# A written-out order of 758 operations over five engines, replaced by another order of the same operations

## The chip, the cores and the metric

The kernel runs on one core of a Trainium2 chip. The metric is the time of one execution on the device in microseconds (us), of which the median of several runs counts; beside it stands one execution taken by the hardware profiler, whose span runs from the first to the last instruction. Five engines work side by side: TensorE (PE in the rows, its weight loads PEld), VectorE (DVE), ScalarE (ACT), GpSimd (POOL) and SyncE (SP), which here only issues transfers. Each engine takes its instructions strictly in the order in which they stand in its own queue and waits at the first whose data or buffer is not ready.

## The reference

Two layers over 2048 positions and 640 channels are computed apart, and their outputs stand side by side (bf16).

```python
# A: a diagonal complex state-space layer
Bu = einsum("bld,pd->blp", x, B_bar)
for t in range(L): h = Lam_bar * h + Bu[:, t]; hs.append(h)
yA = 2 * einsum("blp,dp->bld", stack(hs), Cmat).real + x * Dskip
# B: a short convolution, a product, a long convolution, a gate
k_shift = sum of 4 shifted copies of k, each times a weight per channel
kv = k_shift * v
yB = q * (causal_conv(kv, ssm_k) + kv * ssm_D)     # by FFT in the reference
```

## The kernel before

The kernel builds a list of 758 operations (`build`, over the classes `PartA` and `PartB`). An operation is one instruction on DVE, ACT or POOL, one transfer on SP, or a block of matmuls on PE that fills a group of the eight PSUM banks; PE blocks are always followed by one eviction on DVE or ACT, which frees the banks. Nothing is scheduled at run time. A string, ORDER, lists every operation once as number, engine letter (T for PE, V for DVE, A for ACT, G for POOL, S for SP) and first PSUM bank. `Program.emit` goes through that string and puts each operation on its engine's queue; where an operation reads or overwrites what another engine wrote, a wait is set on that one. So the string decides three things: the order in each queue, which engine does an operation that several could do, and which banks a block takes.

The buffers are fixed places in one array and most are used several times. Those that matter here:

- KT holds one 128-channel plane of k at a time, so the load of the next plane (line 769) waits for the last of the four taps of the one before.
- VT holds three planes of v. Its first columns are scratch for two sine tables before that, so the first load of v waits for the ScalarE sine of line 304.
- KV holds one half (320 channels) of the product k_shift * v, spread anew; H0 holds first the first half of the filter ssm_k, then the scan of part A, then the second half of the filter, then half of q.

Part A. The input is projected in blocks by 512-column matmuls on PE: `up2`, `up1` and `up0` (lines 554 to 620, ten, five and fifteen groups), which reduce 16 consecutive positions to one. A coarse scan over 128 steps runs in two halves on DVE (`coarse`, lines 640 to 660; each half needs two small PE blocks, L646 and L647, and ends with the addition of line 660). Then the states go down again (`down`, L677 and L679, the addition by DVE at L697, or by an identity matmul L677 with a copy by ACT at L695). The output matrix is scaled on PE into CT (`scale_C`, ten blocks, L544, evicted at L548); it needs the two transposed loads of C (L530). Then 16 row blocks are projected (`project`): a load of x (L705), a product with Dskip (L706, DVE or POOL), 20 matmuls of 320 columns (L714, called a projection below), an addition on DVE (L716) and a store (L720).

Part B, in two halves. For each of five planes of 128 channels, k and v are loaded transposed (L769), four taps are multiplied (L197 on DVE, L198 on ACT) and added (L795), the sum is multiplied with v (L796), and the plane is stored to a scratch tensor in HBM, `kv_rows` (L802). The *relay* reads half of that back in the other layout with four transfers (L812). The filter half is loaded by four transfers (L762) and gets ssm_D added (L764). Both then go through a two-stage transform on PE: stage one (`s1`, L832, ten blocks, evicted at L837), stage two (`s2`, L850, eleven or twelve blocks, evicted at L863). The products of the two transforms run on DVE and POOL in four rounds per half (lines 874 to 881; each half's last line-879 subtraction is the end of its products). The inverse goes through `r2` (L895, ten blocks per half, evicted at L900) and `r1` (L916, six blocks per half), whose results are multiplied with the loaded q (L780) by DVE at L928 and stored (L940). Sine tables for the transforms are made early or late on POOL (integer products, L288 and L327) and ACT (L293, L329), and scaled at L197 or L198.

Of the kernel before, what the change touches and what calls it, by code (L numbers as in the profile page):

```python
# [1030 lines left out]
def plain_order(P):  # L1031
# [19 lines left out]
    "135S0 6G0 0G0 7V0 123A0 48V0 84V0 108G0 82V0 458V0 73G0 460G0 459V0 122A0 11V0 50S0 1G0 134S0 42G0 2V0 18G0 8V0 120T4 461G0 "  # L1051
    "20V0 49S0 51S0 121T3 127S0 115G0 12V0 9V0 71G0 26V0 470G0 45V0 44V0 14V0 19V0 21V0 43V0 124T6 126S0 10V0 471G0 53T4 54V4 125V6 "
    "55A0 4A0 114S0 56V0 163T1 137S0 15G0 3V0 74G0 63V0 72G0 64V0 109G0 65V0 119V0 46V0 16V0 57V0 66V0 136S0 60A0 67V0 62A0 85V0 "
    "59A0 87V0 47A0 68V0 5V0 86V0 61A0 69V0 70V0 165T3 75G0 164A1 76G0 77G0 330S0 78G0 79G0 110G0 80A0 58A0 22A0 167T0 166V3 133S0 "
    "81V0 465G0 25V0 104V0 175T6 168A0 33G0 132S0 24V0 118A0 27V0 105V0 333A0 177T2 128S0 332V0 83V0 91V0 28V0 269V0 23V0 334V0 "
    "173T0 129S0 178A2 335V0 176A6 88V0 336V0 331S0 199T2 29V0 89V0 337A0 34G0 90V0 174A0 30G0 169T5 341S0 92V0 94V0 338V0 31G0 "
    "200A2 112A0 179T1 141S0 339V0 170A5 36G0 35A0 116S0 171T4 180A1 93V0 138S0 96V0 343V0 37G0 344A0 52S0 183T2 342S0 101A0 172A4 "
    "345V0 39G0 107V0 191T6 346A0 139S0 40G0 117S0 38A0 347V0 140S0 215T4 32A0 111G0 130S0 41A0 184V2 348A0 181T0 216V4 131S0 192A6 "
    "142V0 466G0 349V0 352S0 157T2 182A0 155T4 207T6 156A4 475G0 158A2 340S0 106V0 145T4 208A6 153T2 185T0 353S0 154V2 146A4 350V0 "
    "355A0 354V0 151T6 224S0 149T4 186A0 95V0 356V0 201T2 152A6 100A0 357V0 97V0 358V0 187T0 202A2 193T6 359V0 98A0 188A0 150A4 "  # L1060
    "102V0 360V0 392S0 99A0 103V0 189T0 194A6 203T2 223S0 190A0 195T6 361V0 204A2 147T4 196A6 143T0 148A4 197T6 144V0 267G0 205T2 "
    "198A6 161T4 206A2 395V0 159T6 270T0 160A6 394V0 217T2 362S0 17V0 396V0 162A4 113A0 397V0 393S0 209T4 398V0 218A2 268V0 271V0 "
    "399V0 272V0 219T2 403S0 210A4 400V0 239T0 220A2 229T6 240A0 221T2 273V0 230A6 231T0 274V0 222A2 211T4 351S0 232A0 241T2 212A4 "
    "237T6 242A2 401V0 213T4 363S0 238A6 233T2 214A4 277V0 243T0 234A2 275T6 406V0 225T4 244A0 276V6 227T2 226A4 235T0 228V2 279T6 "
    "365S0 236A0 249T4 278V0 364S0 245T0 281V0 250A4 280V6 259T2 246A0 260V2 247T4 366S0 265T6 248A4 251T0 405V0 257T2 252A0 266V6 "
    "253T4 402S0 254A4 282V0 261T0 258V2 262A0 255T5 283V0 263T2 256A5 264A2 371T0 407V0 369T6 375T4 372A0 385T2 370V6 376A4 284T0 "
    "386A2 285V0 379T4 288T6 286V0 380A4 381T0 287V0 373T2 408V0 289A6 387S0 374V2 382A0 389S0 409G0 367T6 377T4 368A6 378V4 383T2 "
    "292T0 384A2 683S0 388S0 290T6 293A0 414T4 291V6 440T2 415A4 418T6 441V2 416T0 390S0 419A6 447T4 410V0 425T2 417A0 448V4 429T6 "
    "684G0 426A2 436T0 678S0 430V6 404S0 437A0 438T3 420V0 427T5 439A3 294T7 449T0 428A5 295V7 296T2 422V0 450A0 391V0 423V0 498T6 "
    "297A2 502T0 421V0 484T4 503A0 685T2 431V0 485A4 424V0 499A6 433V0 488T6 686V2 434G0 451T0 489A6 490T4 452V0 687S0 302T2 491A4 "  # L1070
    "298T0 303V2 494T6 299A0 500T4 495A6 496T0 411V0 680T2 703S0 497A0 693S0 679V0 566S0 501A4 412V0 462A0 442V0 413S0 486T0 492T4 "
    "463A0 695T6 567S0 694V0 487A0 444V0 681V2 493A4 445V0 464A0 544T2 696V6 568S0 304T0 569S0 545A2 453V0 308T4 305A0 562T6 309V4 "
    "697S0 550T2 454G0 563A6 560T0 682S0 551A2 561V0 546T4 548T6 547A4 556T2 549V6 554T0 557A2 443G0 558T4 555V0 552T6 713S0 559A4 "
    "564T2 688S0 553A6 565V2 572T0 584T4 573V0 580T6 585A4 455G0 570T2 581V6 571A2 586T0 300T4 587A0 576T2 301V4 306T6 577A2 476G0 "
    "574T0 307V6 588T4 575A0 578T2 457V0 582T6 589A4 715T0 579A2 714V0 432V0 583A6 456V0 435G0 590T4 716V0 627T6 591A4 592T2 628V6 "
    "717S0 594T0 698S0 593A2 623T4 595V0 605T6 624A4 689V0 601T2 603T0 446V0 606A6 316T4 596V0 472A0 690T6 602A2 317V4 604A0 704V0 "
    "467A0 598V0 612T2 614T0 599V0 700T4 615A0 691V6 477A0 607V0 613A2 699V0 324T0 701V4 616T2 325A0 597V0 702S0 625T6 312T4 609V0 "
# [79 lines left out]
```

## Time and profile before

| | |
|---|---|
| median of three runs | 216.62 us (212.32 to 216.9) |
| the profiled execution's own time | 211.25 us |
| its span, first to last instruction | 209.5 us |
| busy share: PE, DVE, ACT, POOL | 87%, 82%, 69%, 33% |
| mean granted TensorE clock | 0.957 of full speed |

The span is shorter than the execution's own time by 1.75 us of start and end around it. All that is read below in microseconds from the start belongs to this one execution.

### The profile page before, as it was taken

How to read it: one execution, taken by the hardware profiler on the slowest of the kernel's cores; microseconds unless marked ns; L12 is line 12 of the kernel's file. 1: busy time of each engine (PE TensorE's matmuls, PEld its weight loads, DVE VectorE, ACT ScalarE, POOL GpSimd, SP SyncE). 2: the span in 40 equal slices, each digit the busy share in tenths (PEclk: the TensorE clock that was granted, in tenths of full speed). 3: DMA queues.
4: the chain of work that ended last, by engine and by line, in shares of the span. 5: the costliest groups of instructions: out<-in, count | busy, mean ns of one | idle time of the engine just before them, and what ended most of it. 6: DMA issues, size and time to landing. Idle time of an engine off the chain costs nothing.

```text
span 209.5 us, 8273 instructions
## 1 busy us (share of the span) xinstructions
PE 181.4 (87%) x3727; PEld 119.0 (57%) x3727; DVE 172.4 (82%) x228; ACT 145.1 (69%) x171; POOL 68.4 (33%) x56
## 2 busy tenths in 40 slices
PE   4699999969999998398769996899999998999960
PEld 1345544524667556376546765576666777677740
DVE  5917998995799999687978997989999989787630
ACT  2099799776959599799957997989889988000000
POOL 8672099950002000016404039450036016102220
PEclk9969999996999999969969999999999999999995
DMA  7999969999999899819961998211096993147685
GB/s 139 176 153 166 199 136 154 159 147 147 223 192 212 234 253 131 173 18 152 136 119 38 210 149 126 69 39 30 34 156 157 186 195 97 35 113 205 156 195 157
DMA packets 107550, 30.20 MB, mean 144 GB/s; under 512 B 102395, under 2 KB 106875, under 8 KB 107515
## 3 DMA queue, kind: packets, MB, share of 16 engines
q1 hardware_dynamic: 107226, 29.35, 81.0%
q8 instruction: 29, 0.48, 1.0%
q10 hardware_dynamic: 288, 0.33, 0.6%
q14 instruction: 7, 0.05, 0.1%
HBM read 10.99 MB, written 7.86 MB: 90 GB/s over the span
## 4 chain that ended last, share of the span: by engine, by line
PE 32%; DMA 20%; DVE 14%; SPq 11%; POOL 5%; issue 4%; ACT 3%; DVEq 0%; ACTq 0%
PE acc L714 16%; DMA arena<-kv_rows 7%; DMA arena<-in_B_ssm_k_dram 6%; DVE arena L795 4%; DMA kv_rows<-arena 4%; PE acc L832 4%; DMA arena<-in_A_x_dram 3%; DVE arena L197 3%; PE acc L679 3%; PE acc L916 3%; SPq L705 2%; POOL arena L288 2%; SPq L762 2%; PE acc L850 2%; PE acc L554 2%
## 5 line engine op out<-in xcount | busy, mean ns | idle before, releaser
L554 PE MATMUL acc<-arena 128*64 128x512 bf16 x400 | 50.5, 407 | 1.6 <-DVE arena L504 1.0
L714 PE MATMUL acc<-arena 128*128 128x320 bf16 x320 | 46.6, 302 | 0.0
L714 PEld LDWEIGHTS <-arena 128*128 128x128 bf16 x320 | 30.5, 99 | 12.8 <-ACT arena L863 0.4
L554 PEld LDWEIGHTS <-arena 128*64 128x64 bf16 x400 | 23.1, 113 | 25.6 <-issue 4.0
L837 ACT CAST arena<-acc 128x1024 bf16<-128x1024 f32 x33 | 31.6, 1026 | 6.7 <-PE acc L832 6.6
L863 ACT CAST arena<-acc 128x960 bf16<-128x960 f32 (+1 forms) x33 | 29.7, 947 | 2.2 <-PE acc L850 1.8
L832 PE MATMUL acc<-arena 64*64 64x64 bf16 x1280 | 15.9, 202 | 11.3 <-DVE arena L764 5.3
L198 ACT ACTIVATE arena<-arena 128x1024 bf16<-128x1024 bf16 (+3 forms) x17 | 21.0, 1242 | 4.4 <-DVE arena L795 4.2
L850 PE MATMUL acc<-arena 128*64 128x160 bf16 x512 | 22.0, 235 | 2.1 <-ACT arena L863 1.0
L832 PEld LDWEIGHTS <-arena 64*64 64x64 bf16 x1280 | 13.4, 114 | 16.3 <-issue 4.9
L850 PEld LDWEIGHTS <-arena 128*64 128x64 bf16 x512 | 17.8, 109 | 6.9 <-ACT arena L863 3.6
L795 DVE TENSOR_TENSOR arena<-arena 128x2048 bf16<-128x2048 bf16 x14 | 20.0, 1429 | 0.7 <-ACT arena L198 0.5
L716 DVE TENSOR_TENSOR arena<-acc,arena 128x640 bf16<-128x640 f32 x16 | 13.2, 823 | 8.4 <-PE acc L714 5.5
L706 POOL TENSOR_TENSOR arena<-arena 128x640 bf16<-128x640 bf16 x6 | 9.2, 1540 | 32.9 <-DMA arena<-in_A_x_dram 32.9
L877 POOL TENSOR_TENSOR arena<-arena 128x1280 bf16<-128x1280 bf16 x4 | 10.3, 2608 | 24.9 <-DVE arena L874 24.9
L900 ACT CAST arena<-acc 128x1024 bf16<-128x1024 f32 x15 | 14.7, 1026 | 1.3 <-PE acc L895 1.2
L837 DVE CAST arena<-acc 128x1024 bf16<-128x1024 f32 x7 | 8.4, 1221 | 6.8 <-PE acc L832 6.6
L679 PE MATMUL acc<-arena 128*128 128x512 bf16 (+2 forms) x50 | 13.5, 334 | 0.3 <-ACT arena L837 0.3
L928 DVE TENSOR_TENSOR arena<-acc,arena 128x960 bf16<-128x960 f32 (+1 forms) x12 | 12.2, 1041 | 1.6 <-PE acc L916 1.4
L697 DVE TENSOR_TENSOR arena<-acc,arena 128x1024 bf16<-128x1024 f32 (+2 forms) x11 | 12.1, 1112 | 1.7 <-PE acc L679 1.2
L795 POOL TENSOR_TENSOR arena<-arena 128x2048 bf16<-128x2048 bf16 x1 | 4.1, 4061 | 27.5 <-DVE arena L197 27.5
L863 DVE CAST arena<-acc 128x640 bf16<-128x640 f32 (+1 forms) x13 | 12.5, 975 | 0.4
(139 smaller groups left out, 289.7 us busy)
## 6 DMA issues: line engine op xcount, KB each, us to landing
out_dram<-arena SPq DMA_DIRECT2D x32, 160.0 KB, 3.4
arena<-in_B_ssm_k_dram SPq DMA_DIRECT2D x8, 320.0 KB, 5.6
kv_rows<-arena SPq DMA_DIRECT2D x5, 512.0 KB, 4.5
arena<-kv_rows SPq DMA_DIRECT2D x8, 320.0 KB, 6.8
arena<-in_A_x_dram SPq DMA_DIRECT2D x16, 160.0 KB, 2.7
arena<-in_B_q_dram SPq DMA_DIRECT2D x8, 320.0 KB, 7.4
arena<-in_A_B_im_dram ACTq DMA_DIRECT2D x1, 160.0 KB, 2.6
arena<-in_A_B_re_dram ACTq DMA_DIRECT2D x1, 160.0 KB, 4.7
```

Source lines behind the costliest of these rows:

```text
L198: self.SM = {nc.scalar: lambda out, in_, by: nc.scalar.mul(out, in_, by), nc.vector: vm(nc.vector), nc.gpsimd: vm(nc.gpsimd)}
L554: e.matmul(o[64 * r:64 * r + 64], lhsT=self.BT[j][:, r, d, :], rhs=self.XP[:, d, 2 * q:2 * q + 2], start=(d == 0), stop=(d == 4), skip_gro ...
L679: e.matmul(B[:, o:o + 128 * k], lhsT=c.RR[:, n, j, :], rhs=A[:, j, q:q + k, 0:128], start=not by_pe, stop=True, skip_group_check=True)
L714: e.matmul(B[:, 512 * b:512 * b + 320], lhsT=lh[j], rhs=self.CT[:, j, 320 * b:320 * b + 320], start=(j == 0), stop=(j == 9))
L716: P.add(f"ev_C{i}", {PDVE: dve(640)}, lambda e, B: e.tensor_tensor(out=ys.rearrange("p (b n) -> p b n", b=2), in0=B.rearrange("p (b n) -> ...
L795: P.add(f"ca{d}_{j}", tt, lambda e: e.tensor_tensor(out=t1, in0=t1, in1=t2, op=ALU.add), outs=[t1], ins=[t1, t2])
L832: e.matmul(B[64 * b:64 * b + 64, 512 * l + 64 * i:512 * l + 64 * i + 64], lhsT=lh[i][ps], rhs=F[ps, b, :], start=True, stop=True, tile_pos ...
L837: P.add(f"e1{what}{hf}_{u}", {PACT: act(1024), PDVE: dve(1024)}, lambda e, B: c.CP[e](out=out, in_=B.rearrange("p (l n k s) -> p k s l n", ...
L850: e.matmul(B[64 * s:64 * s + 64, 512 * b + 160 * i:512 * b + 160 * i + 160], lhsT=c.W[:, k, 64 * b:64 * b + 64], rhs=self.AS[hf][:, k, 160 ...
L863: c.CP[e](out=out, in_=b.rearrange("p r (k j n) -> p r k j n", k=n, j=4) if nj > 1 else b.rearrange("p r (k x) -> p r k x", k=n))
L900: P.add(f"er2{hf}_{u}", {PACT: act(1024), PDVE: dve(1024)}, lambda e, B: c.CP[e](out=out, in_=B.rearrange("p (s n b) -> p b s n", s=2, n=4 ...
L928: e.tensor_tensor(out=Q, in0=B.rearrange("p (g x) -> p g x", g=2)[:, :, 0:80 * n].rearrange("p g (x n) -> p g x n", n=40), in1=Q, op=ALU.mult)
```

## The change

Only ORDER differs: the same 758 operations, each once, in the same buffers, in another order. 88 of the operations that two or three engines could do sit on another engine than before (for instance two more stage-two evictions of the first filter half on ACT), the number of operations per engine is nearly the same, and PE gets nine identity matmuls less, because eight of the `down` additions go from ACT to DVE and five from DVE to ACT. No function differs. The string's first line, cut:

```diff
 ORDER = (
-    "135S0 6G0 0G0 7V0 123A0 48V0 84V0 108G0 82V0 458V0 73G0 460G0 459V0 ...
+    "48V0 18G0 50S0 119G0 123A0 465G0 49S0 122A0 51S0 6G0 137S0 1G0 7V0 ...
```

What this does to the queues shows at three places.

First the transfer queue of SP, from the load of the second B block of part A (L489) to the first filter quarters (L762); L522 loads x for part A, L769 a plane of k or v, L350 the Dskip row. Before:

```order
L489 DMA_TRANSPOSE arena<-in_A_B_re_dram 128x5x256
L489 DMA_TRANSPOSE arena<-in_A_B_im_dram 128x5x256
L769 DMA_TRANSPOSE arena<-in_B_v_dram 128x2048
L769 DMA_TRANSPOSE arena<-in_B_k_dram 128x2048
L762 DMA arena<-in_B_ssm_k_dram 32x80x64
L750 DMA arena<-in_B_ssm_D_dram 4x80
L762 DMA arena<-in_B_ssm_k_dram 32x80x64
L350 DMA arena<-in_A_Dskip_dram 128x640
```

And after:

```order
L489 DMA_TRANSPOSE arena<-in_A_B_im_dram 128x5x256
L489 DMA_TRANSPOSE arena<-in_A_B_re_dram 128x5x256
L522 DMA_TRANSPOSE arena<-in_A_x_dram 128x5x256 x2
L762 DMA arena<-in_B_ssm_k_dram 32x80x64
L522 DMA_TRANSPOSE arena<-in_A_x_dram 128x5x256
L769 DMA_TRANSPOSE arena<-in_B_k_dram 128x2048
L522 DMA_TRANSPOSE arena<-in_A_x_dram 128x5x256
L769 DMA_TRANSPOSE arena<-in_B_v_dram 128x2048
L762 DMA arena<-in_B_ssm_k_dram 32x80x64
```

The first plane of v stood ahead of the second plane of k; now it stands behind it, and behind four transfers of x and a quarter of the filter.

Second, the same queue around the first relay (L802 stores a plane of the product, L812 reads a quarter of a half back, L530 loads C). Before:

```order
L769 DMA_TRANSPOSE arena<-in_B_k_dram 128x2048
L530 DMA_TRANSPOSE arena<-in_A_C_re_dram 128x5x640
L802 DMA kv_rows<-arena 128x2048
L769 DMA_TRANSPOSE arena<-in_B_v_dram 128x2048
L769 DMA_TRANSPOSE arena<-in_B_k_dram 128x2048
L802 DMA kv_rows<-arena 128x2048
L812 DMA arena<-kv_rows 32x80x64 x4
L802 DMA kv_rows<-arena 128x2048
L762 DMA arena<-in_B_ssm_k_dram 32x80x64 x2
```

And after:

```order
L350 DMA arena<-in_A_Dskip_dram 128x640
L769 DMA_TRANSPOSE arena<-in_B_k_dram 128x2048
L530 DMA_TRANSPOSE arena<-in_A_C_im_dram 128x5x640
L802 DMA kv_rows<-arena 128x2048 x3
L812 DMA arena<-kv_rows 32x80x64
L769 DMA_TRANSPOSE arena<-in_B_v_dram 128x2048
L812 DMA arena<-kv_rows 32x80x64
L750 DMA arena<-in_B_ssm_D_dram 4x80
L812 DMA arena<-kv_rows 32x80x64 x2
L769 DMA_TRANSPOSE arena<-in_B_k_dram 128x2048
L762 DMA arena<-in_B_ssm_k_dram 32x80x64 x2
```

Three plane stores now stand together right behind the second load of C, and the relay no longer stands behind the fifth plane of k; one load of v stands between its quarters.

Third, ScalarE from the last evictions of the scaled C (L548) through stage two of the first filter half (L863) and stage one of the first k half (L837); L695 are copies of `down`, L198 a tap. Before:

```order
L548 CAST arena<-acc 128x2x320 x4
L863 CAST arena<-acc 128x2x3x4x40 x8
L837 CAST arena<-acc 128x64x2x8 x4
L695 CAST arena<-acc 128x5x128
L837 CAST arena<-acc 128x64x2x8 x3
L695 CAST arena<-acc 128x4x2x128
L863 CAST arena<-acc 128x2x3x160
```

And after:

```order
L548 CAST arena<-acc 128x2x320 x4
L863 CAST arena<-acc 128x2x3x4x40 x2
L863 CAST arena<-acc 128x2x2x4x40
L863 CAST arena<-acc 128x2x3x4x40 x7
L837 CAST arena<-acc 128x64x2x8 x5
L695 CAST arena<-acc 128x5x128
L837 CAST arena<-acc 128x64x2x8 x3
L198 ACTIVATE arena<-arena 128x2048
L863 CAST arena<-acc 128x2x3x160 x2
```

ScalarE now does ten of the eleven stage-two evictions instead of eight, eight of the ten stage-one evictions instead of seven, and a tap of the fifth plane in between.

Of the other moves the prediction uses these. On PE one projection (row block 1) now stands ahead of the second filter half's stage one, where it stood inside it. On POOL the scaling of a sine table (L197) that stood between two Dskip products ahead of the first `r1` is gone; ACT and DVE do all of them. Near the end four projections are the last blocks on PE, where two matmul blocks of `r1` and projections alternated, and the last two loads of x stand behind a store of the second half of part B.

## Rows read from the trace of the kernel before

**Rows 1.** The page's first part: engine, busy us, share of the span, instructions.

```profile
PE 181.4 (87%) x3727; PEld 119.0 (57%) x3727; DVE 172.4 (82%) x228; ACT 145.1 (69%) x171; POOL 68.4 (33%) x56
```

**Rows 2.** Timeline of PE: start, us, what, and idle time before it with its releaser.

```profile
47.65 0.80 PE L832 MATMUL acc<-arena 64*64 64x64 bf16 x64 [2.30 <-DVE arena L764]
48.38 3.92 PE L554 MATMUL acc<-arena 128*64 128x512 bf16 x20
...
53.30 2.45 PE L554 MATMUL acc<-arena 128*64 128x512 bf16 x20
...
72.75 0.74 PE L544 MATMUL acc<-arena 64*64 64x320 bf16 x16
...
88.59 1.64 PE L832 MATMUL acc<-arena 64*64 64x64 bf16 x128 [2.73 <-DMA arena<-kv_rows]
...
106.69 1.50 PE L832 MATMUL acc<-arena 64*64 64x64 bf16 x96 [2.96 <-DVE arena L764]
...
129.88 1.29 PE L832 MATMUL acc<-arena 64*64 64x64 bf16 x128 [1.62 <-DMA arena<-kv_rows]
...
178.50 0.80 PE L916 MATMUL acc<-arena 64*64 64x80 bf16 x67 [1.19 <-issue]
```

**Rows 3.** Timeline of DVE: start, us, what, idle before it.

```profile
15.93 1.23 DVE L571 CAST arena<-acc 128x1024 bf16<-128x1024 f32 x1 [4.28 <-PE acc L554]
...
38.32 3.60 DVE L434 TENSOR_TENSOR arena<-arena 128x1280 bf16<-128x1280 bf16 x1
41.85 2.91 DVE L795 TENSOR_TENSOR arena<-arena 128x2048 bf16<-128x2048 bf16 x1
...
48.56 1.48 DVE L434 TENSOR_TENSOR arena<-arena 128x1280 bf16<-128x1280 bf16 x1
53.56 1.23 DVE L837 CAST arena<-acc 128x1024 bf16<-128x1024 f32 x1 [3.52 <-PE acc L832]
...
63.65 1.22 DVE L796 TENSOR_TENSOR arena<-arena 128x2048 bf16<-128x2048 bf16 x1
```

**Rows 4.** Timeline of the SP queue: start and length of each issue.

```profile
28.44 2.20 SPq L769 DMA_TRANSPOSE arena<-in_B_k_dram  x1
...
63.25 3.51 SPq L530 DMA_TRANSPOSE arena<-in_A_C_re_dram  x1
...
74.28 0.57 SPq L802 DMA_DIRECT2D kv_rows<-arena  x1
...
92.90 2.98 SPq L762 DMA_DIRECT2D arena<-in_B_ssm_k_dram  x2
```

**Rows 5.** DMA issues by line: us from issue to landing stands last.

```profile
arena<-in_A_x_dram SPq DMA_DIRECT2D x16, 160.0 KB, 2.7
...
arena<-in_B_v_dram SPq DMA_TRANSPOSE x5, 6.2
...
arena<-in_A_C_re_dram SPq DMA_TRANSPOSE x1, 6.9
```

**Rows 6.** The chain that ended last, in order of time: start, us, what.

```profile
81.51 6.84 DMA arena<-kv_rows
...
98.34 7.70 DMA arena<-in_B_ssm_k_dram
```

**Rows 7.** Timeline of ACT, and of POOL.

```profile
79.87 7.89 ACT L863 CAST arena<-acc 128x960 bf16<-128x960 f32 x8 [0.21 <-PE acc L850]
...
40.54 3.14 POOL L327 TENSOR_TENSOR arena<-arena 128x1024 int32<-128x1024 int32 x1
```

**Rows 8.** DVE alone in one stretch (length, busy), then a group of its instructions (mean ns).

```profile
92.74:168.78 76.04, 69.51 (x78) 0.98 0.66 115
...
L837 DVE CAST arena<-acc 128x1024 bf16<-128x1024 f32 x7 | 8.4, 1221 | 6.8 <-PE acc L832 6.6 <-ACT arena L695 0.2
```

**Rows 9.** Who waited for whom: us in total, times, longest.

```profile
DVE arena L764 <- DMA arena<-in_B_ssm_k_dram: 1.5, 1, 1.5
...
DVE arena L697 <- PE acc L679: 1.2, 1, 1.2
```

72 rows, old and new, of the table ORDER are left out of this document.

## The prediction

> **What bounds the kernel now.** I read the page's first part, then PE's timeline with its waits, then the chain that ended last, and last the queues of the engines for which PE waits. The busy shares come first: PE 181.4 of 209.5 us, DVE 172.4 [rows 1]. Both are near full, so an order can only win back waits, and a wait that PE loses is won only if DVE, which evicts, multiplies and adds beside it, can follow. The reader is to see two things.
>
> PE has five waits of over a microsecond behind the start [rows 2]: 2.30 for the first filter half (DVE L764), 2.73 for the first relay from kv_rows, 2.96 for the second filter half, 1.62 for the second relay, and 1.19 inside the first `r1` blocks, which the row puts to issue, that is to nothing that the profile shows: 10.8 together. A wait also costs behind its end, since the clock falls: 20 matmuls of L554 took 3.92 right behind the first wait and 2.45 for the same 20 at full clock [rows 2], another 1.47.
>
> DVE has two long waits ahead of the relay, 4.28 and 3.52, and is stretched where POOL multiplies integers: a spread of L434 took 3.60 beside POOL's L327 of 3.14, and 1.48 alone; a sum of 128x2048 took 2.91, where the product of that shape takes 1.22 [rows 3, 7]. Later it is DVE that is full: from the end of the coarse scan to the last product of the second half it was busy 69.51 of 76.04 us [rows 8]. What follows the last product (all of the second half's `r2`, `r1` and seven projections) is nearly the same work in both orders, so the kernel's end moves as the last product moves, unless PE comes later still.
>
> **The conv chain up to the third plane, on DVE.** The parameter loads now lead the SP queue and the spreads of L434 stand ahead of the taps, so the 4.28 go. The eviction for which DVE waited 3.52 now stands behind one that PE has done by then, so the 3.52 go. Against that, the first plane of v is moved behind the second plane of k on the SP queue, which must wait for the last tap of the first plane. That was at 28.44 [rows 4]; I keep it, because DVE starts earlier but does two more spreads first. Issuing k takes 2.20, one x about 1.6 (an estimate between the 0.5 and the 3.5 that issues here take), so v goes out at 32.2, and lands 6.2 later [rows 5], at 38.4. DVE comes to the product that needs it at about 33: it came to it just behind that last tap, at 30, and has now an eviction (1.23) and two short waits more in front. A new wait of 5.3, then, with all of the second plane queued behind it. It has a cover for something else: POOL's integer products run in that time, so the stretches (3.60 less 1.48, and 2.91 less 1.22: 3.8) go too. Sum: 4.28 + 3.52 + 3.8 less 5.3 = 6.3 earlier. The third product ended at 63.65 + 1.22 = 64.9 [rows 3]; now at 58.6.
>
> Beside POOL's product the spread lost 3.60 - 1.48 = 2.12 [rows 3, 7]. Two of the four products of L327 stood in the first ten microseconds, beside small DVE work, and stand later now; I take nothing for them, since DVE has waits there too; the other end is 2.12 each. The Trainium skill (GPSIMD Engine Reference, section Specifications) says that GpSimd shares its SBUF interfaces with VectorE and contends with DVE instructions that have two SBUF inputs; the 3.60 against 1.48 agree. If that met both products in full, the sum below would be 4.2 smaller, no gain at all; by my reading it stays.
>
> **The first relay and the scaled C, on SP and PE.** In SP's queue one plane store stood behind the fifth plane of k and went out at 74.28, and the relay behind it; its last quarter landed at 81.51 + 6.84 = 88.35 [rows 4, 6]. Now three stores stand together behind the second load of C, with the v load between the quarters. The C load went out at 63.25 [rows 4]; in the new queue a plane store less stands ahead of it, but SP waits some 4 longer for k buffers, so I take 61.6, between 60 and 67. Stores follow at 65, the first quarter when a store has landed (69), the last at 78: it lands at 85, 3.4 earlier.
>
> PE gets there with another wait. It reached the first block of scaled C at 72.75 [rows 2]. One `up0` block of 20 matmuls (2.45 [rows 2]) now stands behind that block; for the smaller blocks that go both ways I take nothing. So 72.75 - 2.45 = 70.3 is the same point of the work, and without the 2.30 and the 1.47 PE comes there at 66.5. The second C load lands at 61.6 + 6.9 = 68.5 [rows 5]: a new wait of 2.0, and a low clock behind it, again 1.47. PE is back at 70.3 less 68.5 less 1.47, a lead of 0.3 (bounds +1.5 and -5, by the C load at 60 or 67). ACT then does ten evictions of stage two instead of eight, at 7.89/8 = 0.99 each [rows 7]: 2 later, half of it covered by the banks that PE still has free. Stage two thus ends on PE at 88.59 - 2.73 - 0.3 + 1.0 = 86.6, the relay has landed, and the 2.73 are gone: PE starts the first k half 2.0 earlier than at 88.59.
>
> **From there to the last product.** SP sent the second filter half at 92.90, the moment the scan freed its place [rows 4]. By DVE alone the scan's end comes 6.3 earlier, at 86.6; but its last swap is a PE block, which stands one group ahead of the end of stage two, at 86.0, and two DVE instructions and the swap itself (1.8, an estimate from a 1.22 and what is shorter) follow: 87.8, 5.1 earlier. The four quarters landed at 98.34 + 7.70 = 106.04 [rows 6], now at 100.9. PE asks for them at about 102, since the projection of row block 1 now stands in front: the 2.96 go, and with the second relay as much earlier the 1.62 too. PE's lead would be 2.0 + 2.96 + 1.62 = 6.6.
>
> DVE's lead is smaller. In the stretch from the scan's end to the last product it now has 82 instructions for 78: three `down` sums, three stage-one evictions, two sums, a tap and two product parts come, four stage-two evictions and three Dskip products go. At 1.22 [rows 8] for the difference of four that is 4.9; as those that go are shorter, I take 6.0. The idle in it was 76.04 - 69.51 = 6.5; of that the waits for the filter (1.5) and for the `down` sums (1.2) [rows 9] and about 1.7 behind PE's late relay go: 2.1 stay. So the last product ends at 87.8 + 69.5 + 6.0 + 2.1 = 165.4, against 92.74 + 76.04 = 168.8: 3.4 earlier. PE could have been 6.6 earlier; the smaller lead counts.
>
> **The end.** Of the 1.19 in `r1`, for which no row names a cause, I take half, 0.6: the POOL scaling in front of that place is gone, but an issue wait can come again (bounds 0 and 1.2). The last two x loads are issued behind a store, close to where they are needed: if each were waited for in full, 2.7 [rows 5], if not, nothing; if the four projections at the end let the stores drain, a gain of 1. I take 0.3 lost. The nine identity matmuls less are on PE, which has the greater lead: nothing.
>
> **The sum.** 3.4 + 0.6 - 0.3 = 3.7 us off the span of 209.5: 205.8, with the 1.75 around it 207.55 for the profiled execution's own 211.25. The median of the runs shown is 216.62, 5.4 above that execution; I take the gain off the median: **212.9 us**, 1.7% less.
>
> **Rivals.**
> No change: DVE's idle in the late stretch stays 6.5, because another order has other waits of the same size. For it: 82 instructions are harder to keep fed than 78, and PE's gaps of 0.1 to 0.5 at evictions come in any order. Against it: the two named waits have their causes moved 5 earlier. The last product at 87.8 + 69.5 + 6.0 + 6.5 = 169.8, 1.0 later, less 0.3: span 210.2, median 217.3.
>
> A larger gain: DVE has no idle there and the kinds that came and went cost only the 4.9: 162.2; then PE's 6.6 and DVE's are one, with 0.3 at the end: span 202.6, median 209.7. For it speaks that only 6.5 of 76 were idle before; against it the C load.
>
> Slower: the first v plane. Each microsecond that it lands later than 38.4 delays everything on DVE behind it, because DVE's queue is in order. At 44.7 the 6.3 are used up, the scan ends at 92.9 as before, and DVE's late stretch then ends at 92.9 + 69.5 + 6.0 + 6.5 = 174.9, 6.1 later: less 0.3, span 215.3, median 222.4. It decides from a landing at about 43, where the gain is gone. For it: the k load ahead waits for a tap on DVE that now has two more spreads in front, and the sine of L304 must have read its scratch. Against it: the DVE starts 4 earlier.
>
> **How the numbers follow.** The forecast 0.44, larger gain 0.18, no change 0.18, slower 0.20. The measurement tells about 2% from no change. The forecast lies near that bound (212.3): 0.22 of it fall beyond, with the larger gain 0.40; same is its other 0.22 and no change's 0.18, 0.40; slower 0.20. The range goes from the larger gain less most of the scatter that the runs show below their median (209.7 - 3.7) to somewhat over half the price of the slower case: 206 to 220. The forecast's own range is 209 to 216.
>
> **What would show it.** Right: PE's row with the first L544 is preceded by a wait of 1 to 4 for the transfer of C; the first relay lands before 86; no wait of PE for L764 over 1; the filter's second half goes out near 88; the last L879 ends near 165. Wrong: v lands after 43, or the filter goes out after 91, or DVE's idle from the scan to the last L879 is over 6, or the last store goes out more than 4 behind the end of PE's last projection.

## The result, and the profile of the changed kernel

The changed kernel takes 204.62 us, the median of four runs (204.28 to 205.41), and is faster: its ratio to the old kernel is 0.9603, with a 95% interval of 0.9531 to 0.9675 (the ratios leave disturbed runs out, so they aren't quotients of the medians). The forecast was 212.9, and the time lies below the low end of the range, 206. The profiled execution took 204.88 with a span of 203.1; 207.55 and 205.8 had been forecast for these two. In the four runs of the old kernel beside it the median is 214.74.

The page's first part, to be read beside [rows 1]:

```profile
PE 181.5 (89%) x3718; PEld 118.6 (58%) x3718; DVE 160.3 (79%) x227; ACT 141.5 (70%) x170; POOL 56.2 (28%) x56
```

PE is busy for the same 181.5 us. All of the 6.4 by which the span is shorter is idle time of PE: 209.5 - 181.4 = 28.1 before, 203.1 - 181.5 = 21.6 now (the busy times are rounded). DVE's busy time has fallen by 12 from its 172.4, though it has only one instruction less; nearly all of that lies ahead of the end of the third plane's product, where 89 instructions were busy for 52.1 before and 89 are for 40.1 now.

PE's timeline at the places of [rows 2]: start, us, what, idle before it with its releaser:

```profile
65.39 0.38 PE L646 MATMUL acc<-arena 128*128 128x512 bf16 x1 [1.06 <-DVE arena L197]
...
66.12 0.64 PE L544 MATMUL acc<-arena 64*64 64x320 bf16 x8 [0.30 <-DMA arena<-in_A_C_im_dram]
66.69 4.05 PE L554 MATMUL acc<-arena 128*64 128x512 bf16 x20
...
84.52 0.44 PE L832 MATMUL acc<-arena 64*64 64x64 bf16 x32
...
99.76 0.77 PE L832 MATMUL acc<-arena 64*64 64x64 bf16 x64
...
121.35 0.44 PE L832 MATMUL acc<-arena 64*64 64x64 bf16 x32
...
169.92 0.23 PE L916 MATMUL acc<-arena 64*64 64x80 bf16 x5 [0.43 <-issue]
```

The three starts of stage one (first relay, second filter half, second relay) have no bracket: the 2.73, 2.96 and 1.62 are gone, and so is the 2.30 for the first filter half. Of the issue wait of 1.19 in `r1`, 0.43 is left. New is the pair of short waits at 65 and 66, and a block of twenty L554 behind them that took 4.05 where 2.45 is usual.

DVE's timeline, for [rows 3]:

```profile
12.78 1.22 DVE L571 CAST arena<-acc 128x1024 bf16<-128x1024 f32 x1 [5.05 <-PE acc L554]
...
37.52 1.93 DVE L796 TENSOR_TENSOR arena<-arena 128x2048 bf16<-128x2048 bf16 x1 [4.97 <-ACT arena L571]
...
57.48 1.23 DVE L796 TENSOR_TENSOR arena<-arena 128x2048 bf16<-128x2048 bf16 x1
...
165.32 0.82 DVE L879 TENSOR_TENSOR arena<-arena 128x1280 bf16<-128x1280 bf16 x1
...
196.99 0.82 DVE L716 TENSOR_TENSOR arena<-acc,arena 128x640 bf16<-128x640 f32 x1 [6.52 <-POOL arena L706]
```

The first wait, which was 4.28, is 5.05 now, but the eviction behind it starts 3.15 earlier. The wait of 4.97 in front of the first plane's product is put to an eviction of ACT that came last by the record, but the load of v landed at 37.4, and that is what DVE waited for. The third plane's product ends at 58.7, the last product at 166.1.

SP's queue, for [rows 4]:

```profile
31.58 2.96 SPq L769 DMA_TRANSPOSE arena<-in_B_v_dram  x1
...
58.53 3.95 SPq L530 DMA_TRANSPOSE arena<-in_A_C_im_dram  x1
62.52 2.02 SPq L802 DMA_DIRECT2D kv_rows<-arena  x3
...
73.84 3.48 SPq L812 DMA_DIRECT2D arena<-kv_rows  x2
...
85.53 1.69 SPq L762 DMA_DIRECT2D arena<-in_B_ssm_k_dram  x2
```

The second C load landed at 66.1. The third quarter of the first relay landed at 80.1; no landing is recorded for the fourth, but the queues moved under 20 GB/s from 80.1 to 80.5, ahead of the next load, so it was there by then (88.35 before). The second filter half went out at 85.53 instead of 92.90.

ACT's row of stage two of the first filter half, for [rows 7], and DVE alone from the filter's issue to the last product, for [rows 8]:

```profile
76.84 9.61 ACT L863 CAST arena<-acc 128x960 bf16<-128x960 f32 x10
```

```profile
85.45:166.14 80.69, 74.64 (x83) 0.98 0.65 120
```

Ten evictions stand back to back, and the chain that ended last runs through them one by one: ACT, not PE, sets the end of stage two, and with it the scan's last swap on PE, which waited for one of these evictions. DVE's late stretch holds 83 instructions and 80.69 - 74.64 = 6.05 idle.

The end: windows from the start of the second half's `r2` to PE's last projection, and from there to the end (length; then busy time of PE, PEld, DVE, ACT and POOL with instructions; granted clock, DMA share, GB/s). Before:

```profile
169.10:202.64 33.54, 31.90 (x845) 24.73 (x844) 24.70 (x27) 7.38 (x8) 9.83 (x6) 1.00 0.61 136
202.64:209.50 6.86, 0.00 (x0) 0.00 (x0) 0.89 (x2) 0.00 (x0) 0.00 (x0) 0.68 0.65 169
```

And after:

```profile
166.28:197.69 31.41, 30.95 (x812) 23.83 (x812) 21.11 (x24) 6.90 (x7) 6.92 (x5) 1.00 0.56 137
197.69:203.10 5.41, 1.04 (x4) 0.31 (x4) 2.08 (x4) 0.00 (x0) 0.00 (x0) 1.00 0.69 188
```

PE needs 2.1 less for the first: 0.95 is work (two `r2` blocks of the first half still stood behind the last product before), 1.2 is idle. The second is 1.45 shorter. In it DVE's last addition ends later behind PE (2.1 against 0.86), but from there to the end it is 3.3 instead of 6.0. The last addition of DVE and the last store of SP before:

```profile
202.68 0.82 DVE L716 TENSOR_TENSOR arena<-acc,arena 128x640 bf16<-128x640 f32 x1 [1.64 <-PE acc L714]
...
204.88 0.93 SPq L720 DMA_DIRECT2D out_dram<-arena  x1
```

And after, where the three stores of A are the only ones left to issue:

```profile
198.25 1.55 DVE L716 TENSOR_TENSOR arena<-acc,arena 128x640 bf16<-128x640 f32 x2
...
199.10 1.33 SPq L720 DMA_DIRECT2D out_dram<-arena  x3
```

### The profile page after: what moved, and what is told of

Its sections match the earlier page's. It is cut to its first block, busy times and chain, and to the rows that moved or that the text cites. A ratio compares the mean times of both kernels' runs of the same rounds, so it can differ in the third digit from the quotient of the medians.

```text
span 203.1 us, 8247 instructions
## 1 busy us (share of the span) xinstructions
PE 181.5 (89%) x3718; PEld 118.6 (58%) x3718; DVE 160.3 (79%) x227; ACT 141.5 (70%) x170; POOL 56.2 (28%) x56
## 4 chain that ended last, share of the span: by engine, by line
PE 39%; DMA 23%; DVE 13%; SPq 9%; ACT 9%; issue 4%; POOL 1%; POOLq 1%; DVEq 0%
PE acc L554 18%; DMA arena<-in_A_x_dram 7%; ACT arena L863 7%; PE acc L714 6%; DMA arena<-in_B_v_dram 4%; DMA arena<-in_A_C_im_dram 4%; PE acc L850 3%; PE acc L895 3%; DMA kv_rows<-arena 3%; DVE arena L697 3%; DMA arena<-in_B_k_dram 3%; SPq L762 3%; DMA out_dram<-arena 2%; SPq L940 2%; PE acc L544 2%
## 5 line engine op out<-in xcount | busy, mean ns | idle before, releaser
L554 PE MATMUL acc<-arena 128*64 128x512 bf16 x400 | 50.2, 407 | 1.4 <-DMA arena<-in_A_x_dram 1.3
L554 PEld LDWEIGHTS <-arena 128*64 128x64 bf16 x400 | 24.2, 113 | 25.3 <-issue 6.6
L863 ACT CAST arena<-acc 128x960 bf16<-128x960 f32 (+1 forms) x39 | 34.9, 932 | 2.7 <-PE acc L850 2.2
L837 ACT CAST arena<-acc 128x1024 bf16<-128x1024 f32 x32 | 31.0, 1026 | 4.0 <-PE acc L832 3.9
L706 POOL TENSOR_TENSOR arena<-arena 128x640 bf16<-128x640 bf16 x9 | 12.5, 1399 | 64.8 <-DMA arena<-in_A_x_dram 46.1
L850 PE MATMUL acc<-arena 128*64 128x160 bf16 x512 | 23.8, 236 | 2.9 <-ACT arena L863 1.2
L795 DVE TENSOR_TENSOR arena<-arena 128x2048 bf16<-128x2048 bf16 x15 | 18.5, 1231 | 1.6 <-ACT arena L198 1.4
L197 DVE TENSOR_SCALAR arena<-arena 128x2048 bf16<-128x2048 bf16 (+3 forms) x21 | 13.4, 654 | 2.7 <-DMA arena<-in_B_k_dram 2.4
L697 DVE TENSOR_TENSOR arena<-acc,arena 128x1024 bf16<-128x1024 f32 (+2 forms) x14 | 14.7, 1073 | 0.8 <-PE acc L679 0.4
L198 ACT ACTIVATE arena<-arena 128x1024 bf16<-128x1024 bf16 (+2 forms) x12 | 14.6, 1217 | 0.1
L895 PE MATMUL acc<-arena 64*128 64x128 bf16 x320 | 11.9, 225 | 0.5 <-DVE arena L879 0.4
L877 DVE TENSOR_TENSOR arena<-arena 128x1280 bf16<-128x1280 bf16 x15 | 12.0, 819 | 0.2
L895 PEld LDWEIGHTS <-arena 64*128 64x128 bf16 x320 | 10.7, 145 | 2.3 <-issue 1.5
```

The source lines that it names most:

```text
L197: vm = lambda e: lambda out, in_, by: e.tensor_scalar_mul(out=out, in0=in_, scalar1=by)
L198: self.SM = {nc.scalar: lambda out, in_, by: nc.scalar.mul(out, in_, by), nc.vector: vm(nc.vector), nc.gpsimd: vm(nc.gpsimd)}
L554: e.matmul(o[64 * r:64 * r + 64], lhsT=self.BT[j][:, r, d, :], rhs=self.XP[:, d, 2 * q:2 * q + 2], start=(d == 0), stop=(d == 4), skip_gro ...
L697: e.tensor_tensor(out=o, in0=b, in1=o, op=ALU.add)
L795: P.add(f"ca{d}_{j}", tt, lambda e: e.tensor_tensor(out=t1, in0=t1, in1=t2, op=ALU.add), outs=[t1], ins=[t1, t2])
L837: P.add(f"e1{what}{hf}_{u}", {PACT: act(1024), PDVE: dve(1024)}, lambda e, B: c.CP[e](out=out, in_=B.rearrange("p (l n k s) -> p k s l n", ...
```

## The experiments

The theory on record: the conv chain and the early relay let the scan end earlier, DVE's lead is carried to the last product, and what follows is worth nothing. The rivals: the gain is made behind the last product; or wherever PE stops waiting. Below, the head is what stands ahead of the second filter half's first load ("filter sent" in the table), the middle goes from there to the last product, and the end is what follows.

| kernel | median us (runs) | ratio to old, 95% | span | filter sent | last product ends | from there to the end |
|---|---|---|---|---|---|---|
| old, first profile | | | 209.5 | 92.9 | 168.8 | 40.7 |
| old_again | 216.45 (1) | | 214.7 | 91.9 | 169.8 | 44.9 |
| new, first profile | 204.62 (4) | 0.9603 [0.9531, 0.9675] | 203.1 | 85.5 | 166.1 | 37.0 |
| new_again | 203.19 (6) | 0.9573 [0.9516, 0.9629] | 200.2 | 83.4 | 164.0 | 36.2 |
| new_head | 207.44 (4) | 0.9746 [0.9663, 0.9829] | 205.5 | 88.1 | 165.8 | 39.7 |
| old_head | 215.32 (4) | 1.0110 [1.0043, 1.0177] | 213.2 | 95.5 | 178.2 | 35.0 |
| old_end | 212.04 (10) | 0.9916 [0.9859, 0.9973] | 210.6 | 86.6 | 167.0 | 43.6 |
| new_end | 213.62 (10) | 1.0035 [0.9949, 1.0122] | 208.5 | 92.2 | 167.2 | 41.3 |
| new_conv | 214.56 (4) | 1.0113 [1.0027, 1.0200] | 212.5 | 96.3 | 172.3 | 40.2 |
| old_c1_ahead | 210.19 (10) | 0.9933 [0.9884, 0.9981] | 207.8 | 92.5 | 168.0 | 39.8 |
| new_x15_first | 202.34 (6) | 0.9546 [0.9477, 0.9615] | 200.5 | 83.4 | 163.3 | 37.2 |
| new_up0_ahead | 203.50 (6) | 0.9600 [0.9559, 0.9641] | 201.2 | 84.1 | 164.4 | 36.8 |
| new_both | 204.25 (6) | 0.9609 [0.9558, 0.9660] | 202.9 | 85.3 | 166.2 | 36.7 |
| new_q1_late | 205.96 (4) | 0.9639 [0.9574, 0.9704] | 202.2 | 85.3 | 164.4 | 37.8 |

Span and what stands behind it come from one profile each. The old kernel ran 210 to 221 us beside new_head, old_head, old_end and new_end (median 213.46), 210 to 215 beside old_again, new_conv, old_c1_ahead and new_x15_first (213.29), and 210 to 215 beside the last four (212.0).

### Which part of the order carries the gain

Each of five hybrids takes the first operations of one order and the rest in the other; evictions of blocks that are open at the seam are put straight behind it. The first tokens behind the seam show it (against the order that it begins with).

new_head:

```diff
...
-389S0 370V4 376A0 377T2 387S0 386A6 378V2 371T0 288T4
+370V4 376A0 386A6 461G0 121T3 466G0 406V0 405V0 402S0
...
```

> The new order up to the first load of the second filter half (349 operations), then the old order for the rest. Theory one (the gain comes from the conv chain, the first relay and the scan that ends earlier): the filter's second half goes out at 85.5 as in the new kernel (92.9 before), the old middle of 76 then ends the last product at about 162 to 165, and with the old end (40.7) the span is 203 to 206, 4 to 6 less than before. Rival (the gain was made behind the last product, or in the middle): under 1.5 less than before.

In SP's queue, and then in DVE's timeline:

```profile
88.13 3.03 SPq L762 DMA_DIRECT2D arena<-in_B_ssm_k_dram  x2
```

```profile
164.99 0.81 DVE L879 TENSOR_TENSOR arena<-arena 128x1280 bf16<-128x1280 bf16 x1
```

The filter went out 2.6 later than expected, the last product ended at 165.8, just past the expected 162 to 165, and the span of 205.5 is theory one's. The head alone brings the last product 3.0 earlier, where the new kernel has 2.6 (first profile; 4.8 in new_again): the lead there is made in the first 88 us. But 39.7 follow, against 37.0, and in the runs the head has 2.5% (1.7 to 3.4) of the new kernel's 4.0%.

old_head:

```diff
...
-387S0 374V2 382A0 389S0 409G0 367T6 377T4 368A6 378V4
+374V2 382A0 476G0 13V0 389S0 377T2 387S0 378V2 683S0
...
```

> The old order up to the first load of the second filter half (365 operations), then the new order for the rest. Theory one: the filter's second half goes out at 92.9 as before; the new middle took 80.6 (85.53 to 166.14), so the last product ends at 170 to 173.5, and with the new end (37.0) the span is 207 to 210.5, within 2.5 of before. Rival (middle and end carry it): span 203 to 205, nearly all of the gain.

Both misjudged it: about 1% slower than the old kernel in the runs, and the last product at 178.2, 9.4 later. Of these 2.6 are a filter that went out at 95.5 instead of 92.9. The other 6.7 are the middle, 82.7 long where the old one has 76.0; 4.6 of that the new middle takes behind its own head too (80.6). So the new middle has none of the gain by itself, it is the longer one, and it doesn't make up for a head that is late. The granted clock was 0.74 from 85 to 100; what the remaining 2.1 hang on isn't shown.

old_end and new_end:

```diff
...
-728S0 464A0 724V0 650T6 468V0 642T4 726V2 651A6 646T0
+724V0 726V2 121T3 464A0 702S0 718S0 720T4 719V0 721V4
...
```

> The new order up to the last product of the second half, then the old order of what is left. If what follows the last product is worth as much as it measured (40.7 before, 37.0 after), the span is 3 to 4 longer than that of the new kernel, about 206.5. By the sum on record (0.3 for the end) it is 0.3 longer, about 203.4.

```diff
...
-722S0 642T2 711V6 506T0 724G0 643A2 514T6 507V0 650T4
+711V6 13V0 514T2 515A2 469A0 506T4 507A4 712S0 725T2
...
```

> The old order up to the last product of the second half, then the new order of what is left. If the new end is worth 3.7 whatever stands ahead, the span is 3 to 4 shorter than before (about 206); if the end's gain hangs on what PE has already done by then (the r2 blocks and the projection of row block 8 or 9), under 1.5; by the sum on record 0.3.

old_end is 7.5 longer than the new kernel, twice what was expected (in the runs the ratios are 0.9916 and 0.9603), but it has a wait at the seam that neither parent has. In DVE's timeline the product of row block 8 waits for its x, and PE's timeline then shows the lost time a second time:

```profile
171.76 0.49 DVE L706 TENSOR_TENSOR arena<-arena 128x640 bf16<-128x640 bf16 x1 [3.44 <-DMA arena<-in_A_x_dram]
```

```profile
182.68 0.91 PE L916 MATMUL acc<-arena 64*64 64x80 bf16 x80 [2.33 <-DVE arena L928]
```

So it doesn't measure the end. new_end is clearer: the new end behind the old middle gains nothing in the runs. Its profile says why: behind the last addition it has 3.1, as the new kernel has 3.3 (6.0 in the old one), but from the last product to that addition it takes 38.2, where the old kernel takes 34.7 and the new one 33.7. It still has the two `r2` blocks to do, two waits of PE with no releaser (0.79 and 1.76), and DVE waits 5.51 for the product with an x that is loaded behind a store. The faster finish is thus a property of the end's order; that it isn't lost again hangs on what has been done before.

new_conv, the new order up to the third plane's product alone:

```diff
...
-395V0 197T6 188A2 351S0 205T4 148A0 396V0 189T2 206A4
+197T6 188A2 205T4 148A0 189T2 206A4 198A6 190A2 461G0
...
```

> The new order only up to the third plane product and what it needs (247 operations), then the old order. Theory one (the conv chain on DVE carries the head's gain): the third product ends at 59 as in the new kernel, the first relay lands near 82, the filter's second half goes out at 88 to 89 and the span is 205.5 to 207. Rival (the relay's place in SP's queue is needed too): the relay lands after 85, the filter goes out after 90, span 208 or more.

The span fell on the rival's side, but not for the rival's reason alone: the third product ended at 64.0, nearly as before (64.9), not at 59. POOL's timeline, then DVE's:

```profile
47.22 4.73 POOL L327 TENSOR_TENSOR arena<-arena 128x1024 int32<-128x1024 int32 x2 [8.14 <-DVE arena L317]
...
53.56 5.04 POOL L327 TENSOR_TENSOR arena<-arena 128x1024 int32<-128x1024 int32 x2
```

```profile
54.06 2.79 DVE L795 TENSOR_TENSOR arena<-arena 128x2048 bf16<-128x2048 bf16 x1
...
56.88 2.54 DVE L197 TENSOR_SCALAR arena<-arena 64x5 f32<-64x5 f32 x2
```

At this seam four integer products of POOL fall beside the taps. The sum took 2.79 where the new kernel's takes 1.22, and of the pair of L197 the scaling of 64x5 alone took 1.75 (0.17 there); POOL's products took 2.4 to 2.5 each instead of 1.90. Where POOL's integer products stand is thus worth about 5 us of DVE's conv chain, and it was nearly the chain's whole lead. The Trainium skill (GPSIMD Engine Reference, section Specifications) names SBUF interfaces shared with VectorE and contention with DVE instructions with two SBUF inputs or in a two-port mode; 2.79 against 1.22 agrees.

### PE's waits and DVE's lead

old_c1_ahead moves one projection of the old order, and exchanges its banks with those of a stage-one block:

```diff
...
-423V0 498T6 297A2 502T0 421V0 484T4 503A0 685T2 431V0 485A4
+423V0 685T4 498T6 297A2 502T0 421V0 484T2 503A0 431V0 485A2
...
```

> The old order with one projection (row block 1) moved ahead of the wait for the filter's second half, so that PE works in the 2.96 for which it waited; DVE's order is untouched. By the step on record (the smaller of the two leads counts, and DVE has none here): last product at 168.8 as before, span within 0.7 of before. Rival (PE's waits count even where DVE leads, since PE does now what it would do behind the last product): PE is 3 earlier behind the filter's first blocks and the span 1.5 to 3 shorter.

PE's timeline:

```profile
103.84 2.88 PE L714 MATMUL acc<-arena 128*128 128x320 bf16 x20
106.65 1.06 PE L832 MATMUL acc<-arena 64*64 64x64 bf16 x96
110.32 0.64 PE L832 MATMUL acc<-arena 64*64 64x64 bf16 x32 [2.61 <-ACT arena L837]
```

The projection fills the wait for the filter, and a wait of 2.61 appears three blocks later: the projection had covered the time in which ACT evicts the first blocks. A wait was moved, not removed. The span of 207.8 is 1.7 below that of the old kernel's first profile, which is the rival's side, but two profiles of the old kernel lie 5.2 apart, and the 0.7% that the runs show is too little to decide between the two theories.

### Why executions of one kernel differ

old_again and new_again repeat the two kernels unchanged.

> The old kernel once more, for a second profiled execution. Its runs go from 209.8 to 220.7. If the executions differ in one place (a relay or filter transfer that lands later), this one shows that place beside the first profile: a wait that is 1 or more longer, and every wait in front of it as long as before. If the difference is spread, no wait differs by over 0.7.

> The new kernel once more, beside the three that change it. In its first profile one block of L554 took 4.05 behind the wait for C, and 2.46 in the profile of the kernel with row block 15 first, which has the same order up to there; everything behind it came 2.1 to 2.8 earlier there. If that block decides between the executions, this profile shows either 2.4 to 2.6 (then the filter goes out near 83.5 and the span is near 200.5) or 3.9 to 4.1 (85.5 and near 203); if it does not, the span goes with neither.

In old_again the last product came 1.0 later than in the first profile, but 4.2 more were lost behind it. PE's timeline there:

```profile
177.03 1.77 PE L895 MATMUL acc<-arena 64*128 64x128 bf16 x51 [1.60 <-issue]
...
181.47 1.30 PE L916 MATMUL acc<-arena 64*64 64x80 bf16 x67 [1.66 <-issue]
182.70 3.99 PE L714 MATMUL acc<-arena 128*128 128x320 bf16 x20
```

Two waits for nothing that the profile shows, 1.60 and 1.66, where the first profile has one of 1.19, and a projection of 3.99 instead of 2.89 behind them, at a granted clock of 0.71. The two longer waits and the slow projection make up 3.2 of the 4.2. So the difference sits mostly in the second half's `r2` and `r1`, not at a relay or a filter transfer.

In new_again it sits where expected. PE's timeline, and ACT's:

```profile
65.28 0.22 PE L647 MATMUL acc<-arena 128*128 128x128 bf16 x1 [0.91 <-DVE arena L197]
65.78 0.47 PE L544 MATMUL acc<-arena 64*64 64x320 bf16 x8 [0.29 <-DMA arena<-in_A_C_im_dram]
66.18 2.45 PE L554 MATMUL acc<-arena 128*64 128x512 bf16 x20
```

```profile
74.73 9.61 ACT L863 CAST arena<-acc 128x960 bf16<-128x960 f32 x10
```

The waits are nearly those of the first profile, but the block took 2.45, not 4.05. PE alone in the block's stretch (length, busy, granted clock, DMA share, GB/s), in the new kernel's first profile and in new_again:

```profile
66.69:70.74 4.05, 4.05 (x25) 0.58 0.89 195
```

```profile
66.18:68.60 2.42, 2.42 (x28) 1.00 0.83 261
```

The granted clock was 0.58 in the one, near the lower of its two levels (1.2 GHz), and 1.00, the upper (2.4 GHz), in the other. ACT's ten evictions start 2.1 earlier (0.5 by which PE came to the block earlier, and the 1.6 of the block), the filter goes out at 83.4 and the last product ends at 164.0: the 2.1 are carried through. But the block isn't all in which executions differ. new_q1_late below has the same order up to there and its block took 2.46 too; PE came to it at 68.00, and the filter went out at 85.3, as late as in the first profile.

### Three attempts to improve, and one on q

new_x15_first, with two swaps near the end:

```diff
...
-664S0 739G0 665S0 677S0 754G0 740T0 756V2 749V0 751V4 121T2
+664S0 754G0 739G0 665S0 677S0 740T0 749V0 751V4 756V2 121T2
...
```

> The new order with two swaps at the end: POOL multiplies row block 15 before row block 12 with Dskip, and DVE adds row block 14 before 15. If the 6.52 for which DVE waits at the end of the new kernel sets its end, that wait falls under 4, the last addition comes 1.0 to 1.3 earlier and the span is 0.9 to 1.3 shorter (about 202). Rival (the stores of B set the end): span as the new kernel's, 203.1, within 0.3.

DVE's timeline, then SP's:

```profile
189.60 0.82 DVE L716 TENSOR_TENSOR arena<-acc,arena 128x640 bf16<-128x640 f32 x1 [1.42 <-PE acc L714]
192.38 0.82 DVE L716 TENSOR_TENSOR arena<-acc,arena 128x640 bf16<-128x640 f32 x1 [1.96 <-PE acc L714]
195.10 0.82 DVE L716 TENSOR_TENSOR arena<-acc,arena 128x640 bf16<-128x640 f32 x1 [1.89 <-PE acc L714]
```

```profile
191.19 3.95 SPq L940 DMA_DIRECT2D out_dram<-arena  x5
195.23 2.10 SPq L720 DMA_DIRECT2D out_dram<-arena  x3
```

The 6.52 fell to three waits for PE's own projections. But SP was still issuing five stores of B until 195.14 and the last three of A straight behind; from the last product to the end it is 37.2, no gain. The shorter span comes from the block of L554, which took 2.46 in this execution.

new_up0_ahead moves a block and its evictions, and changes the banks of it and of three small blocks:

```diff
...
-398V0 270T2 227T6 217T4 362S0 399V0 228A6 146A0
+398V0 217T6 270T2 227T4 362S0 399V0 146A0 218A6 228A4
...
```

> The new order, with the last up0 block (20 matmuls of L554 and what belongs to it) moved ahead of PE's wait for the scan's first swap and for C, so that PE works where it waited 1.06 and 0.30. If that wait and the low clock behind it cost what they measured (1.4 and 1.6), L554's last 20 take 2.4 to 2.6, the filter goes out at 83 to 84 and the span is 2 to 3 shorter than the new kernel's 203.1. Rival (DVE's chain alone sets the scan's end, as the step on record has it): filter at 85.5, span within 0.5.

```profile
64.09 1.32 PE L554 MATMUL acc<-arena 128*64 128x512 bf16 x10
65.83 1.33 PE L554 MATMUL acc<-arena 128*64 128x512 bf16 x10 [0.42 <-issue]
...
69.17 0.44 PE L832 MATMUL acc<-arena 64*64 64x64 bf16 x32 [0.80 <-ACT arena L548]
```

PE's timeline has lost the wait for C and the slow block, and has 0.42 inside the block and 0.80 for ACT instead, which had nothing to evict for 1.48 while the long block ran. Its span is below the new kernel's first and above its second profile, and its median is that of new_again (203.5 and 203.19): no gain.

new_both has the two edits above:

```diff
...
+398V0 217T6 270T2 227T4 362S0 399V0 146A0 218A6 228A4
...
+664S0 754G0 739G0 665S0 677S0 740T0 749V0 751V4 756V2 121T2
...
```

> The two swaps at the end (row block 15 first) and the up0 block ahead of the wait, together. If both prices stand it is the fastest of all: span 199.5 to 201, median 201 to 202.5. If the swaps at the end are worth nothing (the stores of B set the end, as the profile of the swaps alone suggests with 37.2 from the last product to the end, 37.0 before them), it equals the kernel with the up0 block alone within 0.4.

It missed: 204.25, not below new_again. No version beats the new kernel by more than the intervals of the ratios.

new_q1_late moves two loads (634, 637) behind the last x load before the end:

```diff
...
-472A0 634S0 715T2 315V0
+472A0 715T2 315V0
...
-479A0 637S0 506T4 629V0
+479A0 506T4 629V0
...
-728S0 464A0
+728S0 634S0 637S0 464A0
...
```

> The new order, with two of the four loads of q's second half moved behind the last x load before the end, so that q is being loaded while PE runs the second half's r2 and the first r1 blocks, as in the old order. If that load is what holds up PE's instructions (gaps of issue of 1.19 in the first profile of the old kernel, 1.60 and 1.66 in the second, 0.4 in the new), the gaps of issue in PE's r2 and r1 blocks sum to over 1.2 and the end from the last product is 0.8 to 2 longer than 37.0. Rival (they hang on PE's own pace): sum under 0.9, end within 0.5.

DVE's timeline, then PE's:

```profile
175.13 0.61 DVE L706 TENSOR_TENSOR arena<-arena 128x640 bf16<-128x640 bf16 x1 [3.92 <-DMA arena<-in_A_x_dram]
```

```profile
176.53 2.12 PE L916 MATMUL acc<-arena 64*64 64x80 bf16 x144 [1.50 <-DVE arena L716]
```

The end is 37.8, within the first expectation, but for another reason: no issue wait appeared, the 1.50 is a wait for DVE, and DVE waited 3.92 for an x that was issued behind the q loads. That q's load causes the issue waits isn't supported by this; the last section has what the traces do show of them.

## Why the prediction was right in kind and wrong in size

**The conv chain: the total right, two of its terms not.** Forecast 6.3 earlier, third product at 58.6; measured 6.2, at 58.7. The load of v was to land at 38.4 with a wait of 5.3; it landed at 37.4 with 4.97. But the 4.28 didn't go, it is 5.05 now, and 1.12 of the 3.52 is left: up to the third product DVE's idle rose from 12.8 to 18.6, where the sum has it fall by 2.5. What paid for that was busy time, 3.8 in the sum and 11.9 measured. The sum counted two places that were stretched beside POOL's integer products, and the old trace has more (a product of 128x2048 took 2.80 at 29.95, products of only 128x20 took 1.75 and 1.87 at 26.81 and 32.67); the mix of instructions differs too, so not all of the 11.9 is POOL's. That two errors of some 8 cancelled is luck. That the stretches by POOL go was right in kind (L434 takes 1.49 on average now, 1.91 before), and new_conv shows that without it nearly all of the chain's lead is gone.

**The wait for C: right place, smaller.** Forecast 2.0 with 1.47 of low clock behind; C landed at 66.1, not 68.5, and PE waited 1.06 (for DVE's small scaling that feeds the scan's swap) and 0.30, not the 1 to 4 for the transfer that were to show it. The slow block came in one profile (1.6) and not in the other.

**The relay and the filter: earlier than forecast.** The relay landed by 80.5, not 85; the filter went out at 85.5 (83.4 in new_again), not 87.8. PE's lead behind C, 0.3 in the sum, was 2.6 (70.3 less 66.12 and the 1.6), so the scan's swap stood at 83.5 instead of 86.0; the 1.8 from there to the filter was 2.0.

**DVE's late stretch: wrong, and it cancelled that.** The sum gave 75.5 busy and 2.1 idle; it was 74.64 and 6.05 (74.34 of 80.56 in new_again). The idle stayed near the 6.5 of the old kernel, as the rival "no change" had it, and just past the bound of 6 named as a sign of error. The filter 2.3 earlier and the stretch 3.1 longer put the last product at 166.1 instead of 165.4. That rival gave 169.8 because it kept 87.8 for the filter. The slower rival (v landing at 44.7) didn't come.

**The end: the step that failed.** "What follows the last product is nearly the same work in both orders, so the kernel's end moves as the last product moves" gave 0.3; it measured 3.7 (40.7 to 37.0). The six profiles of the new order, unchanged or with a small edit, have 36.2 to 37.8, and the six of orders with the old end 39.7 to 44.9, so it isn't one execution's accident. The work wasn't the same: the old order has two `r2` blocks of the first half behind the last product and the new one has them ahead (0.95); it is the order of PE's own queue that puts them there, not PE's lead. The issue wait went from 1.19 to 0.43 and other gaps with it (1.2 in all). And the last part is 1.45 shorter, because the stores drain faster: from DVE's last addition to the end it is 5.4 to 6.6 in the six profiles with the old end and 3.0 to 4.6 in the eight with the new one. The sum named this term, "a gain of 1" if the four projections let the stores drain, and set it below the two x loads; DVE did wait 6.52 there, but only 1.25 of the drain's 2.7 was lost by it. new_end shows that the order of the end alone doesn't give the whole. new_head has 1.0 of it, less than two profiles of the old kernel differ by.

**The median: the larger error.** "I take the gain off the median" took the shown 216.62, 5.4 above the old kernel's profiled execution, as if the new kernel had the same excess. It has none (204.62, and 204.88 profiled). Of the 8.3 between 212.9 and 204.62, 2.7 are the span's (207.55 to 204.88) and 5.6 this step. Eleven later runs of the old kernel had a median of 212.0; two of the three shown were long ones. The measured ratio of 0.9603, taken off the 216.62, would give 208.0.

## What to carry to other kernels

Count PE's idle over the whole span, not its lead at one point: an order can put PE's blocks ahead of a late event that DVE sets, and then less stands behind it. And count the stores that are still to go out behind the last addition. A sum that comes out can hold errors that cancel; compare it term by term. A piece of a good order isn't good by itself: of five hybrids one kept over half of its gain, and of the others one was seen to lose it to POOL beside DVE and one to an x load at the seam. Take a forecast off the runs that resemble the profiled execution, and ask where the others lose their time before adding it to a kernel that may not have that place.

## What was not expected

A wait of 1.06 and 0.30 was followed by a block of 4.05 in one execution, one of 0.91 and 0.29 by 2.45 in another of the same kernel, and the 1.6 between them reached the last product in full (166.1 and 164.0). The order alone doesn't decide that block.

In the old kernel's `r2` and `r1` PE lost 1.19 in one execution and 1.60 + 1.66 in another to waits with no releaser in the profile; new_end shows one too, in PE's timeline:

```profile
186.79 0.30 PE L916 MATMUL acc<-arena 64*64 64x80 bf16 x11 [1.76 <-issue]
```

The traces hold a likely cause, which no experiment here tested. The page lists a queue `q8 instruction` with 29 packets of 16 KB; by their number (some 7440 matmuls and weight loads, so 256 to a packet) they are PE's instructions. All 22 issue waits of PE over 0.6 in the fourteen traces end 1.2 to 1.6 behind the end of such a packet; for the four above, which end at 178.5, 177.0, 181.5 and 186.8, the packet ended at 176.9, 175.6, 179.9 and 185.5. Two packets end at least 3.3 apart, and 128 matmuls of L916 with their weight loads take 1.34, so in dense blocks of small matmuls PE can run out of instructions.

A scaling of 64x5 on DVE, 0.17 by itself, took 1.75 beside POOL's integer products, and the sum of 128x2048 lost as much (2.79 less 1.22): it isn't the size of the DVE operation that sets what it loses.
